# Softmax-free attention mixed with a state-space convolution: the denominators of the last stage in a PSUM bank, with copies in SBUF

## The chip, the cores and the metric

The kernel runs on one core of a Trainium2 chip. The metric is the device time of one launch in microseconds (us). Before the change the median of three runs was 179.49 us (179.27 to 180.06).

The engines go by their short names in the profile: PE is TensorE (its weight loads are a row of their own, PEld), DVE is VectorE, ACT is ScalarE, POOL is GpSimd and SP is SyncE, which only issues DMAs here. A suffix q (ACTq, SPq) marks what the engine's sequencer does, such as issuing a DMA. Each engine works through its own list of instructions in order.

## The reference

The input x has 2048 rows of 448 numbers. Two branches are computed and mixed per row:

```
g   = sigmoid(x . gate_w)
q, k, v = split(x @ wqkv) into 16 heads of 28
phi(t)  = (t + 1 if t > 0 else exp(t)) + 1e-6
kv  = sum over rows of phi(k)^T v          # 28 x 28 per head
z   = sum over rows of phi(k)              # 28 per head
a   = (phi(q) @ kv) / (phi(q) . z + 1e-6) @ wo
b   = long convolution of x along the rows (S4D kernel) + x * D_skip
out = g * a + (1 - g) * b
```

The denominators of this case are the 16 numbers `phi(q) . z + 1e-6` of every row, one per head.

## The kernel before, in words

The rows are cut into 16 blocks of 128 (`NC = 16`); a block lies with its rows on the 128 partitions. All instructions are written out in the order in which each engine is to do them (`manual_schedule`), so the order of the Python lines that name one engine is that engine's order. Tile pools decide only the buffers: a tile with the tag of an earlier one waits until the last reader of that one is done.

The first part (to line 507) takes block after block: project k, make phi(k), accumulate the products `g` of phi(k) with x in four PSUM banks, project q, make phi(q) (`pq`), and the convolution branch `y`. While the last block passes, z is summed over the partitions by a matmul and copied to `zb` (L629).

Then comes a bridge (L630 to L741). ACT copies the four banks `g` to SBUF (`gs`, L646). PE multiplies them with the weights of v (L691, in two parts `k` and `tr`; each part goes through the four copies in turn for one block of heads, then through them again for the next), DVE masks the result (`kv`), ACT and DVE split it into a high and a low half, and PE multiplies with wo (L671, tiles m0 to m3). ACT takes the high half of each m (`m_high`, L675, into `wk` or `shl`), DVE the low half (L679). Four small DMAs move rows of `shl` into `wk` (L725, L726); one of them is issued from ACT's list.

The last stage is a loop over the 16 blocks (L766 to L789). For block c:
- `norm_a` (L517): POOL multiplies `pq` with `zb` into `prod`, two buffers.
- `norm_b` (L522): DVE sums `prod` over the 28 columns of each head, into `den`.
- `norm_d` (L527, L529): DVE adds 1e-6, multiplies with `e1` (from the gate) and takes the reciprocal, in the loop for two blocks at once, in every second pass.
- `norm_c` (L540, L543, L546): `pn` is `pq` times the reciprocals; POOL does two pieces, DVE a small one of 48 columns.
- `turn_pe`, `turn_split` (L577, L584, L585): PE transposes `pn`, ACT takes the high half `th`, DVE the low half.
- `tail` (L588): ACT copies three gate rows of `rows` into the tile of `th`.
- `attend` (L602): PE multiplies the halves with `wk` and `rc`, 11 matmuls; the eighth takes `rc` and the rows that `tail` copied.
- `final_b`, `final_c` (L607, L609, L613): DVE adds `y`, SP sends the block out, ACT keeps a copy of the bank in `pq`.

`norm_bd(0)` to `norm_bd(3)` (reduce, then L527 and L529 for one block) and `norm_c(0)` to `norm_c(2)` stand in the bridge, between the pieces named above. The gates for the last stage are transposed by `gates_b` (L564) into a PSUM bank, copied by ACT (L567) and DVE (L568).

Of the kernel before, what the change touches and what calls it, by code (L numbers as in the profile page):

```python
# [7 lines left out]
F32 = mybir.dt.float32  # L8
# [3 lines left out]
ALU = mybir.AluOpType  # L12
AX = mybir.AxisListType
PSUM = bass.MemoryType.PSUM

P = 128
S = 2048
D = 448
H = 16
DH = 28  # L20
N = 256
NC = S // P
# [14 lines left out]
DS = 12  # L37
# [93 lines left out]
def gated_mix_kernel(ctx: ExitStack, tc: tile.TileContext, xin, wq_d, wv_d, wo_d, abc_d, ldt_d, dsk_d,  # L131
                     tri_d, ident_d, mask_d, gcat_d, sel_d, first_d, gin_d, lag_d, out):
    nc = tc.nc
    PE, ACT, DVE, POOL, SP = nc.tensor, nc.scalar, nc.vector, nc.gpsimd, nc.sync
# [39 lines left out]
    tp = work.enter_context(tc.tile_pool(name="tp", bufs=2))  # L174
    ps = work.enter_context(tc.tile_pool(name="ps", bufs=1, space=PSUM))
# [18 lines left out]
    o = 0  # L194
    for part in PARTS:
# [8 lines left out]
        o = e  # L204
# [305 lines left out]
    gs = [gs[i // 2][:, i % 2] for i in range(4)]  # L510
    mh, ml = wkh, wkl
    rc = []
    pn, th, tl, pd, dn = {}, {}, {}, {}, {}

    def norm_a(c):
        pd[c] = tp.tile([P, D], F32, name="prod", tag="pk")
        POOL.tensor_tensor(out=pd[c], in0=pq[:, c], in1=zb, op=ALU.mult)  # L517

    def norm_b(c):
        if c % 2 == 0:  # L520
            dn[c // 2] = tp.tile([P, 2, H], F32, name="den", tag="den", bufs=3)
        DVE.tensor_reduce(out=dn[c // 2][:, c % 2], in_=pd.pop(c).rearrange("p (h d) -> p h d", h=H), op=ALU.add,  # L522
                          axis=AX.X)

    def norm_d(c, n):
        r = dn[c // 2][:, c % 2:c % 2 + n]
        DVE.scalar_tensor_tensor(out=r, in0=r, scalar=1e-6, in1=e1[:, c:c + n, None].to_broadcast([P, n, H]),  # L527
                                 op0=ALU.add, op1=ALU.mult)
        DVE.reciprocal(out=r, in_=r)  # L529

    def norm_bd(c):
        norm_b(c)
        norm_d(c, 1)

    def norm_c(c):
        n = pn[c] = tp.tile([P, J, P], F32, name="pn", tag="pn")
        r = dn[c // 2][:, c % 2]
        a = pq[:, c, :3 * DJ].rearrange("p (j h d) -> p j h d", j=3, h=4)
        b = pq[:, c, 3 * DJ:].rearrange("p (h d) -> p h d", h=4)
        POOL.tensor_tensor(out=n[:, :3, :DJ].rearrange("p j (h d) -> p j h d", h=4), in0=a,  # L540
                           in1=r[:, :H - 4].rearrange("p (j h) -> p j h", j=3)[:, :, :, None].to_broadcast([P, 3, 4, DH]),
                           op=ALU.mult)
        DVE.tensor_tensor(out=n[:, :3, DJ:].rearrange("p j (h d) -> p h j d", h=4),  # L543
                          in0=b[:, :, :DS].rearrange("p h (j d) -> p h j d", j=3),
                          in1=r[:, H - 4:, None, None].to_broadcast([P, 4, 3, DS // 3]), op=ALU.mult)
        POOL.tensor_tensor(out=n[:, 3].rearrange("p (b h d) -> p b h d", b=2, h=4),  # L546
                          in0=b[:, None, :, DS:].to_broadcast([P, 2, 4, DH - DS]),
                          in1=r[:, None, H - 4:, None].to_broadcast([P, 2, 4, DH - DS]), op=ALU.mult)
# [11 lines left out]

    def gates_b(g, tag):
        n = g.shape[1]
        o = ps.tile([P, 512], F32, name="o2", tag="v1")
        PE.transpose(o[:n, :P], g, ident)  # L564
        w = tp.tile([P, D], F32R, name="phs", tag=tag)[:n, :3 * P].rearrange("p (i t) -> p i t", i=3)
        phs.append(w)
        ACT.copy(w[:, 0:2], o[:n, None, :P].to_broadcast([n, 2, P]))  # L567
        return lambda: DVE.tensor_tensor(out=w[:, 2], in0=o[:n, :P], in1=w[:, 0].bitcast(F32), op=ALU.subtract)  # L568
# [46 lines left out]
    c = NC - 2  # L615
# [18 lines left out]
    g2 = gates_a(1, NC - 1)  # L634
    POOL.memset(rows[DT:RX, :2 * D], 0.0)
    last = gates_b(g2, "pkl")
    DVE.tensor_copy(okn, zo[:1, D:D + 1])
    norm_bd(0)
    norm_c(0)
    last()  # L640
    norm_a(2)
    norm_bd(1)
    norm_c(1)
    for i in range(4):
        do_g(c + 1, (i,))
# [80 lines left out]
    SP.dma_start(out=mh[DT:, 3].bitcast(F32), in_=shl[:DT, 1].bitcast(F32))  # L726
    o0 = turn_pe(0)
    norm_c(2)
    norm_a(4)
    mrows(0, p3, "a")  # L730
# [11 lines left out]
    def late():  # L742
        c = NC - 1
        yield 5
        e = tp.tile([P, D], F32, name="e", tag="e")
        t = tp.tile([P, D], F32, name="t", tag="t")
        ACT.activation(e1[:, c:], qo[:, D:D + 1], AF.Exp, scale=-1.0)
        ACT.activation(e, qo[:, :D], AF.Exp)
        yield 6
        DVE.tensor_scalar(out=e1[:, c:], in0=e1[:, c:], scalar1=1.0, scalar2=None, op0=ALU.add)  # L750
        DVE.tensor_scalar(out=t, in0=e, scalar1=1.0, scalar2=1e-6, op0=ALU.min, op1=ALU.add)
        DVE.reciprocal(out=og[:, c:], in_=e1[:, c:])
        yield 7
        DVE.tensor_scalar(out=og[:, c:], in0=og[:, c:], scalar1=-1.0, scalar2=1.0, op0=ALU.mult, op1=ALU.add)
        DVE.scalar_tensor_tensor(out=pq[:, c], in0=qo[:, :D], scalar=C1, in1=t, op0=ALU.add, op1=ALU.max)
        yield 8
        g = gates_a(c, NC)
        yield 9
        last = gates_b(g, "e")
        yield 10  # L760
        last()
        phi(c)
# [3 lines left out]
    for c in range(NC):  # L766
        if c % 2 and c + 4 < NC:
            norm_d(c + 3, 2)
        if c:
            final_b(c - 1)  # L770
        if 0 < c < NC - 2:
            norm_c(c + 2)
        if c + 1 < NC:
            turn(c + 1)
        if c:
            final_c(c - 1)
        if c + 1 < NC:
            tail(c + 1)
        if c + 6 < NC:
            norm_a(c + 6)  # L780
        if c + 5 < NC - 1:
            phi(c + 5)
        attend(c, ((0, D // 2), (D // 2, D)) if c == NC - 1 else ((0, D),))
        if c == 0:
            norm_b(4)
        if c + 5 < NC:
            norm_b(c + 5)
        if c == due:
            due = next(later, None)  # L789
# [94 lines left out]
```

## Time and profile before

| | |
|---|---|
| median of three runs | 179.49 us (179.27 to 180.06) |
| the profiled execution | 179.93 us |
| its span | 178.1 us |
| PE busy | 172.5 us, 97% |
| DVE busy | 115.9 us, 65% |
| ACT busy | 94.7 us, 53% |
| POOL busy | 119.5 us, 67% |

The span runs from the first to the last recorded instruction; 1.83 us of the profiled execution lie outside it. Rows of the timeline read: start in us, busy time in us, engine, line, operation, output tile, input tiles, count, and in brackets the idle time of that engine just before and what ended it. Buffer numbers are left out of the names. The chain of work that ended last is PE for 91% of the span.

### The profile page before, as it was taken

How to read it: one execution, taken by the hardware profiler on the slowest of the kernel's cores; microseconds unless marked ns; L12 is line 12 of the kernel's file. 1: busy time of each engine (PE TensorE's matmuls, PEld its weight loads, DVE VectorE, ACT ScalarE, POOL GpSimd, SP SyncE). 2: the span in 40 equal slices, each digit the busy share in tenths (PEclk: the TensorE clock that was granted, in tenths of full speed). 3: DMA queues.
4: the chain of work that ended last, by engine and by line, in shares of the span. 5: the costliest groups of instructions: out<-in, count | busy, mean ns of one | idle time of the engine just before them, and what ended most of it. 6: DMA issues, size and time to landing. Idle time of an engine off the chain costs nothing.

```text
span 178.1 us, 2750 instructions
## 1 busy us (share of the span) xinstructions
PE 172.5 (97%) x879; PEld 152.0 (85%) x879; DVE 115.9 (65%) x238; ACT 94.7 (53%) x212; POOL 119.5 (67%) x124
## 2 busy tenths in 40 slices
PE   6999999999999999999999999999999999999991
PEld 2598999999999999999989999877879999899990
DVE  1747647688857173562824519389799999998551
ACT  3779388884537244372536653444565455564441
POOL 3167577879259969687598999059289998773100
PEclk9999999999999999999999999999999999999999
DMA  5999974198003303033033000000031221131222
GB/s 166 416 291 271 249 203 153 10 375 239 4 1 118 118 0 120 5 118 101 18 118 122 0 0 0 0 4 5 6 60 68 88 98 62 67 119 73 109 76 82
DMA packets 7784, 18.40 MB, mean 103 GB/s; under 512 B 1755, under 2 KB 4520, under 8 KB 7768
## 3 DMA queue, kind: packets, MB, share of 16 engines
q1 hardware_dynamic: 7720, 18.16, 32.2%
q8 instruction: 7, 0.11, 0.3%
q10 hardware_dynamic: 48, 0.06, 0.2%
q14 instruction: 9, 0.07, 0.1%
HBM read 14.20 MB, written 3.67 MB: 100 GB/s over the span
## 4 chain that ended last, share of the span: by engine, by line
PE 91%; DVE 5%; issue 1%; ACT 1%; ACTq 0%
PE g L388 20%; PE q L319 19%; PE a L602 16%; PE k L319 15%; PE v L319 6%; PE tr L577 3%; PE q L246 3%; PE v L396 2%; PE v L395 2%; PE m L671 1%; DVE th L585 1%; DVE ot L607 1%; DVE den L527 1%; DVE den L522 1%; PE tr L691 1%
## 5 line engine op out<-in xcount | busy, mean ns | idle before, releaser
L602 PE MATMUL a<-wk,th 128*128 128x448 f32 (+1 forms) x170 | 39.5, 364 | 0.0
L388 PE MATMUL g<-pkh,xn 128*128 128x448 f32 x112 | 36.1, 370 | 0.0
L602 PEld LDWEIGHTS a<-wk,th 128*128 128x128 f32 x170 | 29.6, 189 | 2.6 <-DMA wk<-shl 0.3
L319 PE MATMUL k<-wk,xt 128*128 128x448 f32 x132 | 30.4, 376 | 0.0
L347 DVE SCALAR_TENSOR_TENSOR k<-k,e 128x448 f32<-128x448 f32 x12 | 7.6, 632 | 33.9 <-ACT e L346 33.9
L319 PE MATMUL q<-wqh,xt 128*128 128x450 f32 x120 | 27.7, 368 | 0.0
L319 PEld LDWEIGHTS k<-wk,xt 128*128 128x128 f32 x132 | 25.1, 190 | 2.9 <-ACT wk L416 0.8
L407 POOL TENSOR_TENSOR y<-y,t 128x448 f32<-128x448 f32 x16 | 18.6, 1163 | 13.4 <-DVE t L400 13.1
L224 POOL TENSOR_TENSOR xn<-xr,xn 128x448 fp32r<-128x448 f32 x16 | 19.2, 1200 | 8.7 <-ACT xn L234 8.4
L319 PEld LDWEIGHTS q<-wqh,xt 128*128 128x128 f32 x120 | 22.7, 189 | 2.7 <-issue 0.7
L517 POOL TENSOR_TENSOR prod<-pq,zb 128x448 f32<-128x448 f32 x16 | 18.6, 1162 | 8.3 <-ACT zb L629 6.0
L388 PE MATMUL g<-pkl,xn 128*128 128x448 f32 x64 | 23.5, 367 | 0.0
L388 PEld LDWEIGHTS g<-pkh,xn 128*128 128x128 f32 x112 | 21.1, 188 | 2.8 <-issue 0.2
L345 ACT ACTIVATE e<-k 128x448 f32<-128x448 f32 x12 | 6.5, 545 | 30.2 <-PE k L319 30.2
L240 POOL TENSOR_TENSOR y<-xr,rows 128x448 f32<-128x448 f32 x16 | 18.7, 1168 | 0.0
L224 POOL TENSOR_TENSOR xt<-xr,xt 128x512 fp32r<-128x512 f32 x14 | 18.3, 1306 | 0.2 <-ACT xt L228 0.2
L540 POOL TENSOR_TENSOR pn<-pq,den 128x336 f32<-128x336 f32 x16 | 12.1, 754 | 7.7 <-DVE den L529 5.6
L584 ACT CAST th<-tr 128x512 fp32r<-128x512 f32 x16 | 9.4, 589 | 9.2 <-PE tr L577 9.0
L607 DVE SCALAR_TENSOR_TENSOR ot<-y,og,a 128x448 f32<-128x448 f32 (+1 forms) x17 | 10.4, 615 | 4.6 <-PE a L602 4.6
L613 ACT COPY pq<-a 128x448 f32<-128x448 f32 (+1 forms) x17 | 8.8, 517 | 6.5 <-DVE ot L607 5.7
L388 PEld LDWEIGHTS g<-pkl,xn 128*128 128x128 f32 x64 | 11.2, 175 | 1.2 <-issue 0.2
L319 PE MATMUL q<-wql,xt 128*128 128x450 f32 x45 | 11.7, 364 | 0.0
(135 smaller groups left out, 305.0 us busy)
## 6 DMA issues: line engine op xcount, KB each, us to landing
xr<-in SPq DMA_DIRECT2D x15, 512.0 KB, 3.5
out<-ot SPq DMA_DIRECT2D x15, 224.0 KB, 1.9
pq<-in SPq DMA_DIRECT2D x4, 448.0 KB, 13.3
y<-in SPq DMA_DIRECT2D x2, 480.0 KB
y<-in SPq DMA_DIRECT2D x2, 450.0 KB, 7.4
wv<-in SPq DMA_DIRECT2D x1, 896.0 KB, 5.5
wo<-in SPq DMA_DIRECT2D x1, 784.0 KB
y<-in SPq DMA_DIRECT2D x1, 448.0 KB
```

What stands on the lines that cost most here:

```text
L224: eng.tensor_tensor(out=o, in0=r, in1=h.bitcast(F32), op=ALU.subtract)
L240: POOL.tensor_tensor(out=y[:, c], in0=plain[c][:, :D], in1=dsk, op=ALU.mult)
L319: PE.matmul(o[:, :n], lhsT=a, rhs=b, start=run.n == 1, stop=not seq)
L347: DVE.scalar_tensor_tensor(out=pks[c], in0=pks[c], scalar=1.0, in1=e, op0=ALU.add, op1=ALU.max)
L388: PE.matmul(g[i][:a.shape[1], :D], lhsT=a, rhs=b, start=c == 0 and n == 0, stop=c == NC - 1 and n == len(seq) - 1)
L407: POOL.tensor_tensor(out=y[:, c], in0=y[:, c], in1=t, op=ALU.add)
L517: POOL.tensor_tensor(out=pd[c], in0=pq[:, c], in1=zb, op=ALU.mult)
L540: POOL.tensor_tensor(out=n[:, :3, :DJ].rearrange("p j (h d) -> p j h d", h=4), in0=a, in1=r[:, :H - 4].rearrange("p (j h) -> p j h", j=3)[ ...
L584: ACT.copy(h, ov)
L602: PE.matmul(a[:, lo:hi], lhsT=u_, rhs=w_[:, lo:hi], start=n == 0, stop=n == 10)
L607: DVE.scalar_tensor_tensor(out=ot[:, lo:hi], in0=y[:, c, lo:hi], scalar=og[:, c:c + 1], in1=a[:, lo:hi], op0=ALU.mult, op1=ALU.add)
L613: ACT.copy(pq[:, c, lo:hi], a[:, lo:hi])
```

## The change

The change has three parts. The sums of all 16 blocks go into one PSUM tile `dp`, in the bank with tag v1, where they stay: the sum, the 1e-6, the gate factor and the reciprocal are computed there. After each reciprocal ACT copies the result into the old SBUF tile `den`, since POOL reads `den` in `norm_c` from SBUF. DVE's small piece of `norm_c` reads `dp`. The transposed gates of `gates_b` move from the bank v1 to the bank q.

```
     def norm_b(c):
-        if c % 2 == 0:
-            dn[c // 2] = tp.tile([P, 2, H], F32, name="den", tag="den", bufs=3)
-        DVE.tensor_reduce(out=dn[c // 2][:, c % 2], in_=pd.pop(c).rearrange("p (h d) -> p h d", h=H), op=ALU.add,
-                          axis=AX.X)
+        if not dp:
+            dp.append(ps.tile([P, 512], F32, name="den", tag="v1")[:, :NC * H].rearrange("p (c h) -> p c h", c=NC))
+        DVE.tensor_reduce(out=dp[0][:, c], in_=pd.pop(c).rearrange("p (h d) -> p h d", h=H), op=ALU.add, axis=AX.X)
 
     def norm_d(c, n):
-        r = dn[c // 2][:, c % 2:c % 2 + n]
+        r = dp[0][:, c:c + n]
         DVE.scalar_tensor_tensor(out=r, in0=r, scalar=1e-6, in1=e1[:, c:c + n, None].to_broadcast([P, n, H]),
                                  op0=ALU.add, op1=ALU.mult)
         DVE.reciprocal(out=r, in_=r)
+        if c % 2 == 0:
+            dn[c // 2] = tp.tile([P, 2, H], F32, name="den", tag="den", bufs=3)
+        ACT.copy(dn[c // 2][:, c % 2:c % 2 + n], r)
...
         DVE.tensor_tensor(out=n[:, :3, DJ:].rearrange("p j (h d) -> p h j d", h=4),
                           in0=b[:, :, :DS].rearrange("p h (j d) -> p h j d", j=3),
-                          in1=r[:, H - 4:, None, None].to_broadcast([P, 4, 3, DS // 3]), op=ALU.mult)
+                          in1=dp[0][:, c, H - 4:, None, None].to_broadcast([P, 4, 3, DS // 3]), op=ALU.mult)
...
-        o = ps.tile([P, 512], F32, name="o2", tag="v1")
+        o = ps.tile([P, 512], F32, name="o2", tag="q")
```

Lines behind the new ones are two higher in the changed kernel (L646 becomes L648, L675 becomes L677, L588 becomes L590). The order of PE, DVE, POOL and SP is the same; ACT has ten copies more (L531).

ACT's list at the start of the bridge, before: the copy of the gates, then the four copies of `g`, then `zs` for another matmul.

```order
L567 CAST phs<-o_1254 14x256 [waits PE_49]
L646 COPY gs_1182<-g_142 128x448 [waits PE_49,Pool_49]
L646 COPY gs_1182<-g_143 128x448 [waits PE_49]
L646 COPY gs_1183<-g_144 128x448 [waits PE_49,Pool_49]
L646 COPY gs_1183<-g_145 128x448 [waits PE_49]
```

The same place after:

```order
L569 CAST phs<-o_1254 14x256 [waits PE_49]
L531 COPY den<-den 128x16 [waits DVE_49] x2
L648 COPY gs_1182<-g_142 128x448 [waits PE_49,Pool_49]
L648 COPY gs_1182<-g_143 128x448 [waits PE_49]
L648 COPY gs_1183<-g_144 128x448 [waits PE_49,Pool_49]
L648 COPY gs_1183<-g_145 128x448 [waits PE_49]
```

The copies of the reciprocals of blocks 0 and 1 stand ahead of the four copies of `g`, and each waits for DVE.

ACT's list later in the bridge, before, from the high half of m3 (`shl`) to the transposed block 1:

```order
L675 CAST shl<-m_1339 112x448 [waits PE_49]
L675 CAST wk_69<-m_1349 112x448 [waits PE_49]
L725 DMA wk_69<-shl 16x2x448 [waits DVE_49]
L675 CAST wk_69<-m_1370 112x448 [waits PE_49]
L675 CAST wk_69<-m_1376 112x448 [waits PE_49]
L584 CAST th<-tr 128x512
L735 CAST wk_69<-shl 64x448
L736 CAST rc<-shl 64x448
L588 CAST th<-rows 48x128 [waits DVE_49,Pool_49]
L584 CAST th<-tr 128x512 [waits PE_49]
```

The same place after:

```order
L677 CAST shl<-m_1342 112x448 [waits PE_49]
L531 COPY den<-den 128x16 [waits DVE_49]
L677 CAST wk_69<-m_1353 112x448 [waits PE_49]
L727 DMA wk_69<-shl 16x2x448 [waits DMAHW6_49,Activation_49]
L677 CAST wk_69<-m_1374 112x448 [waits PE_49]
L677 CAST wk_69<-m_1380 112x448 [waits PE_49]
L586 CAST th<-tr 128x512
L737 CAST wk_69<-shl 64x448
L738 CAST rc<-shl 64x448
L531 COPY den<-den 128x16 [waits DVE_49]
L590 CAST th<-rows 48x128 [waits Pool_49]
L586 CAST th<-tr 128x512 [waits PE_49]
```

The copy for block 2 stands ahead of the high half of m2, of ACT's DMA and of all that follows; the copy for block 3 stands ahead of the rows of block 0 (L590).

DVE's list in the loop for the second pass (c = 1), after; in the program before, the row of `pn` there has no wait:

```order
L526 SCALAR_TENSOR_TENSOR den<-den,e_60 128x32 [waits DVE_49]
L528 RECIPROCAL den<-den 128x32 [waits DVE_49]
L609 SCALAR_TENSOR_TENSOR ot<-y,og,a 128x448 [waits PE_49]
L545 TENSOR_TENSOR pn<-pq,den 128x4x3x4 [waits Activation_49]
L587 TENSOR_TENSOR th<-tr,th 128x512 [waits Activation_49]
```

DVE's piece of `pn` now waits for ACT's copy out of the same bank, which in turn waits for the reciprocal.

More of the change, by code (lines that the diff above doesn't have):

```diff
@@ L512, in gated_mix_kernel @@
     rc = []
-    pn, th, tl, pd, dn = {}, {}, {}, {}, {}
+    pn, th, tl, pd, dn, dp = {}, {}, {}, {}, {}, []
     def norm_a(c):
```

## The prediction

> **What bounds the kernel now.** I read the summary first, then the stretches of the last stage, then the chain of work that ended last.
>
> ```profile
> PE 172.5 (97%) x879; PEld 152.0 (85%) x879; DVE 115.9 (65%) x238; ACT 94.7 (53%) x212; POOL 119.5 (67%) x124
> ...
> 145.00:150.00 5.00, 5.00 (x30) 4.56 (x29) 5.00 (x12) 3.09 (x8) 4.60 (x7) 1.00 0.26 96
> 150.00:155.00 5.00, 4.77 (x27) 4.13 (x26) 4.96 (x13) 2.13 (x5) 3.50 (x5) 1.00 0.12 46
> ...
> 151.93 0.56 DVE pn L543
> 152.49 0.14 issue
> 152.62 0.63 PE tr L577 x4
> ```
>
> PE is busy 97% of the span, so whatever holds PE is paid in full, and whatever only frees another engine is paid back only where PE stands idle. In the last stage DVE is full as well (5.00 of 5.00 us from 145 to 150). Only once does it show: from 150 to 155 PE is busy 4.77 of 5.00 us, and the chain names the place, the transposes of block 9, which start at 152.62 because DVE's piece of `pn` ended late. That stall is 0.23 us.
>
> **What the change removes.** DVE's small operations on `den` have long and short instances.
>
> ```profile
> L527 DVE SCALAR_TENSOR_TENSOR den<-den,e x10: 170/358/1073, 119.5 to 160.9; 128x32 f32<-128x32 f32 x6, 128x16 f32<-128x16 f32 x4
> L543 DVE TENSOR_TENSOR pn<-pq,den x16: 194/534/1165, 120.3 to 167.0; 128x48 f32<-128x48 f32 x16
> ```
>
> The same 48 columns take 194 ns or 1165 ns; 16 or 32 columns take 170 to 1073 ns. The longest L527 stands beside a product of POOL:
>
> ```profile
> 149.78 1.30 POOL L517 TENSOR_TENSOR prod<-pq,zb 128x448 f32<-128x448 f32 x1 [0.20 <-DVE e L750]
> ...
> 150.06 1.07 DVE L527 SCALAR_TENSOR_TENSOR den<-den,e 128x32 f32<-128x32 f32 x1
> ```
>
> It ends at 151.13, when the product has just ended (151.08). So I read the long ones as held by POOL's instructions on two SBUF operands; with `dp` in PSUM they have one SBUF input left. DVE operations that read one PSUM and one SBUF operand show no such spread in this stage (L607, L585: 0.58 to 0.69 us each), so I take the short times for all: 10 x (358 - 170) + 16 x (534 - 194), by medians, is some 7 us of DVE time. Of this PE can get back the 0.23 us at 152.62 and hardly more; DVE's freed time beyond it is time in which DVE waits for PE. The gain is bounded by zero and the idle time of PE and its weight loads in this stage, 0.8 us (this stall, and 0.25 and 0.34 us at 130.8 to 131.4, shown below, which the profile puts down to a copy and a DMA). I take 0.23.
>
> **What the change adds: a first hold on ACT.** Ten copies alone are small. Their nearest rows are these, a PSUM source with one column and an SBUF source with 128:
>
> ```profile
> L365 ACT ACTIVATE e<-q x14: 162/171/177, 20.7 to 115.4; 128x1 f32<-128x1 f32 x14
> L588 ACT CAST th<-rows x16: 294/295/297, 130.7 to 171.0; 48x128 fp32r<-48x128 f32 x16
> ```
>
> A copy of 16 or 32 columns lies between 0.17 and 0.295 us; I take 0.20, near the row from PSUM. But each waits for a reciprocal, ACT works in order, and the first two stand ahead of the four copies of `g` that PE needs.
>
> ```profile
> 119.44 2.19 ACT L646 COPY gs<-g 128x448 f32<-128x448 f32 x4 [0.29 <-PE g L388]
> 119.53 0.45 DVE L527 SCALAR_TENSOR_TENSOR den<-den,e 128x16 f32<-128x16 f32 x1
> 120.01 0.25 DVE L529 RECIPROCAL den<-den 128x16 f32<-128x16 f32 x1
> 120.30 0.21 DVE L543 TENSOR_TENSOR pn<-pq,den 128x48 f32<-128x48 f32 x1
> 120.42 0.27 DVE L568 TENSOR_TENSOR phs<-o,phs 14x128 fp32r<-14x128 f32 x1
> 120.62 0.60 DVE L522 TENSOR_REDUCE den<-prod 128x16 f32<-128x448 f32 x1
> 121.25 0.45 DVE L527 SCALAR_TENSOR_TENSOR den<-den,e 128x16 f32<-128x16 f32 x1
> 121.74 0.25 DVE L529 RECIPROCAL den<-den 128x16 f32<-128x16 f32 x1
> 122.14 1.73 PE L691 MATMUL k<-gs,wv 128*112 128x112 f32 x16
> 123.70 1.74 PE L691 MATMUL tr<-gs,wv 128*112 128x112 f32 x16
> 124.23 0.20 DVE L704 TENSOR_TENSOR kv<-k,mask 112x48 f32<-112x48 f32 x1
> ```
>
> Before, ACT starts `gs` at 119.44 and is done at 121.63, just ahead of PE's use at 122.14. After, block 0: 119.53 + 0.17, reciprocal 0.25, the gaps of 0.03 to 0.05 us between dependent rows, and the copy 0.20 end at 120.2; DVE's `pn`, which now waits for that copy, starts no later than its old 120.30, so the reduce of block 1 stays at 120.62 (its `prod` is there only at 119.94 anyway). Block 1: 121.25 + 0.17 and 0.25 give 121.70, the copy ends at 121.95. The saving of 0.28 us on DVE is in this. Then `gs`: 121.95 + 2.19 = 124.14 instead of 121.63, 2.5 us late. PE takes 16 passes in (123.70 - 122.14) = 1.56 us, 0.098 us each, two for a product; the fourth copy is first needed by passes 7 and 8, so ten passes lie behind it: 124.19 + 0.98 = 125.17 for the start of `tr`, against 123.70. **PE is 1.47 us late**, and the DVE and ACT work on kv behind it with it, since it starts when PE ends.
>
> [...]
>
> **A second hold.** Block 2's copy stands ahead of the high half of m2.
>
> ```profile
> 126.74 0.54 ACT L675 CAST wk<-m 112x448 fp32r<-112x448 f32 x1
> ...
> 127.53 0.71 ACTq L725 DMA_DIRECT2D wk<-shl  x1
> ...
> 128.27 0.25 DVE L529 RECIPROCAL den<-den 128x16 f32<-128x16 f32 x1
> 128.28 0.97 ACT L675 CAST wk<-m 112x448 fp32r<-112x448 f32 x2 [1.00 <-DVE den L527]
> ...
> 129.13 0.60 ACT L584 CAST th<-tr 128x512 fp32r<-128x512 f32 x1
> ...
> 129.96 0.68 DVE L585 TENSOR_TENSOR th<-tr,th 128x512 fp32r<-128x512 f32 x1
> ...
> 130.56 0.61 DVE L679 TENSOR_TENSOR wk<-m,wk 112x448 fp32r<-112x448 f32 x1
> 130.73 0.29 ACT L588 CAST th<-rows 48x128 fp32r<-48x128 f32 x1
> 130.80 0.30 PEld L602 LDWEIGHTS a<-wk,th 128*128 128x128 f32 x2 [0.25 <-ACT rc L736]
> ...
> 131.09 0.60 DVE L522 TENSOR_REDUCE den<-prod 128x16 f32<-128x448 f32 x1
> 131.44 0.91 PEld L602 LDWEIGHTS a<-wk,th 128*128 128x128 f32 x5 [0.34 <-DMA wk<-shl]
> 131.77 1.16 POOL L517 TENSOR_TENSOR prod<-pq,zb 128x448 f32<-128x448 f32 x1 [0.86 <-DVE den L522]
> 131.94 0.25 DVE L529 RECIPROCAL den<-den 128x16 f32<-128x16 f32 x1
> ...
> 132.37 0.19 PEld L602 LDWEIGHTS a<-rc,th 112*128 112x128 f32 x1
> ```
>
> The reciprocal of block 2 ended at 128.52; 1.47 later is 129.99. Copy 0.25 with its wait: the high half of m2 starts at 130.24, not 126.74 + 1.47 = 128.21, and ends at 130.78. Then comes ACT's DMA, whose issue holds ACT for 0.71 us, and the next high half starts at 131.53 instead of 128.28: ACT is 3.25 late, DVE's `th` of block 0 starts at 133.01 instead of 129.96 (3.05), the low half and the reduce behind it likewise, and the reciprocal of block 3 ends at 132.19 + 3.05 = 135.24. Its copy ends at 135.49, and only then may ACT copy the rows for block 0: 135.5 + 0.29 = 135.8 (130.73 before). PE's eighth matmul of block 0 needs them: weight load at 135.9 instead of 132.37. **PE is 3.5 us late**, 1.47 of it from the first hold, 2.0 from the second. The DMA alone (issue at 130.8, 3.27 us late against 127.53) would hold PE's second matmul, near 131.0 before, to 134.3, which is covered.
>
> POOL adds a little. It waits for the reduce of block 3 (0.86 us at 131.77) and then for that of block 4, behind the `th` of block 1; its `pn` of block 3, just in time for PE before (135.87 for 135.91), comes some 3.7 late. I add 0.2.
>
> **The rest.** In the loop the copies stand ahead of `th` in every second pass, behind a reciprocal; DVE has L607 (0.58) to do until its `pn` needs the copy (0.25), so this costs PE nothing as long as DVE keeps the ease that the first part gives. The gates in the bank q are read off at 120.69, and the q matmuls behind them start at 121.83: 1.1 us of cover. The bank v1 is free when DVE's reduce first writes it. After 136 the order is as before and PE is full, so nothing gives the delay back except the 0.23 us.
>
> **Sum:** 1.47 + 2.0 + 0.2 - 0.23 = 3.5 us (rounded). On the profiled execution, 179.93, this is 183.4; it lies 0.44 above the median of the runs, so on the median 179.49 + 3.5 = **183.0 us**. Copies of 0.17 to 0.295 us (three on the path), the gap to POOL and the DMA move this to 182.4 to 183.9.
>
> **Rivals.**
> - Only the first hold reaches the end: `wk` and the rows have more room than I see, and PE's q matmuls (2 us from 128.3) hide the second. For it: before, ACT waited 1.00 us for nothing but its own DMA there. Against it: PE already waited for DMA and `rc` at 130.8 and 131.4. 179.49 + 1.47 - 0.23 = 180.7. Chance 0.14.
> - The other side, not slower: DVE's freed 7 us starts work earlier than PE's stalls show, and the bridge's stalls of 0.25 and 0.34 us go too. It decides if block 1's reciprocal were ready by 119.44, when ACT starts `gs`; against it, `prod` of block 1 ends at 119.94. 179.49 - 0.8 = 178.7, and a little lower if PE has idle time that the rows hide. Chance 0.05; without any hold and with the 0.23 alone, 179.3, chance 0.04.
> - A third hold in the loop: DVE's `pn` waits for ACT's copy out of the same bank. [...] If the copy falls behind `th` (0.59 us) or `pq`, six passes lose some 0.2 us each: 184.2. It decides where DVE's work of two passes, some 4.9 us, passes PE's two blocks of 2.69 us (5.38). Chance 0.12.
> - The change doesn't do what it says: the long instances stay long with a PSUM operand. Then block 1's copy is 0.28 later, the 0.23 stays, and a full DVE adds to it: 184 us. Chance 0.07.
>
> **Chances and range.** My forecast has 0.58, the rivals 0.42. Faster by over 0.5% (0.9 us, about what a measurement of this kernel can tell from no change) has 0.03, the lower part of the second rival; within it 0.06, the rest of that rival and the 179.3; slower 0.91. The range reaches to the first rival below and the third above: 180.7 to 184.3.
>
> **What would show it.** In the profile after: `gs` starting near 122.0 behind two copies L531; the first product of `tr` near 125.2; the high half of m2 near 130.2; the weight load of `rc` near 135.9 with ACT's row copy ahead of it; the transposes of block 9 without a wait for DVE; L526 and L545 all near 0.2 us. I am wrong if ACT reaches `gs` before 121, if PE has idle time after 140 that I don't name, or if the end moves by less than the bridge does.

## The result and the profile after

The changed kernel takes 182.59 us, the median of four runs (182.25 to 183.19); the kernel before took 179.63 (179.27 to 180.06) beside it. The ratio is 1.0175 [1.0157, 1.0193], with the 95% interval in brackets: slower by 2.8 to 3.5 us.

The summary of the changed kernel, and the three stretches of its last stage that answer to the ones shown of before (columns: stretch, its length, busy time of PE, PEld, DVE, ACT and POOL with instruction counts, granted clock, DMA share, GB/s):

```profile
PE 173.1 (96%) x879; PEld 151.9 (84%) x879; DVE 110.3 (61%) x238; ACT 95.5 (53%) x222; POOL 119.4 (66%) x124
```

```profile
130.00:135.00 5.00, 3.56 (x18) 2.55 (x17) 3.33 (x8) 3.30 (x8) 3.04 (x5) 1.00 0.22 49
145.00:150.00 5.00, 5.00 (x30) 4.58 (x29) 4.14 (x9) 3.04 (x10) 5.00 (x8) 1.00 0.25 92
150.00:155.00 5.00, 5.00 (x29) 4.56 (x28) 4.53 (x15) 2.73 (x7) 4.32 (x7) 1.00 0.27 95
```

The reader sees both halves of the change here. DVE is relieved: 110.3 us busy against 115.9, no longer full from 145 to 150, and PE has no gap from 150 to 155, where it had one. The price is paid from 130 to 135, at the end of the bridge, where PE is busy 3.56 of 5.00 us.

DVE's small operations of the changed kernel, each line with its shortest, median and longest instance, and ACT's ten copies:

```profile
L526 DVE SCALAR_TENSOR_TENSOR den<-den,e x10: 176/183/200, 119.0 to 162.8; 128x32 f32<-128x32 f32 x6, 128x16 f32<-128x16 f32 x4
L545 DVE TENSOR_TENSOR pn<-pq,den x16: 191/196/205, 119.7 to 169.1; 128x48 f32<-128x48 f32 x16
L531 ACT COPY den<-den x10: 172/185/187, 119.5 to 163.4; 128x32 f32<-128x32 f32 x6, 128x16 f32<-128x16 f32 x4
```

The long instances are gone: L526 reaches 200 ns where L527 reached 1073, L545 reaches 205 where L543 reached 1165.

The chain of work that ended last, in the changed kernel, begins in the bridge (start, us, what):

```profile
129.73 0.50 issue
130.23 0.97 ACT wk L677 x2
131.20 0.49 ACT th L586
...
131.75 0.57 issue
132.32 0.61 DVE wk L681
132.94 0.55 DVE den L522
...
134.22 0.29 ACT th L590
...
137.75 0.52 DVE ot L609
138.26 0.12 DVE pn L545
138.38 0.14 issue
138.52 0.63 PE tr L579 x4
```

Before, the chain could be followed back through the whole program, and PE was 91% of the span. Now it can be followed back to 129.73 only; ACT and DVE carry it by turns from there to 138.5, and PE takes over at the transposes of block 3. That is the stretch in which the time is lost.

**A common zero.** In the profiled run of the changed kernel all of the bridge starts 0.53 us earlier than before, as ACT's copy of `zb` shows (first row before, second row after):

```profile
117.07 0.53 ACT L629 COPY zb<-zo 128x448 f32<-128x448 f32 x1 [1.07 <-PE zo L627]
```

```profile
116.54 0.53 ACT L631 COPY zb<-zo 128x448 f32<-128x448 f32 x1 [1.07 <-PE zo L629]
```

That copy starts between 116.42 and 117.24 in the fourteen profiles of this study, though only one edit touches the code ahead of it; it is the scatter of the first part. So I subtract its start from every time. This table has, from that zero, the weight load of `rc` for block 0 (PE's eighth matmul), the transposes of block 3, the pitch from the transposes of block 8 to those of block 9, the start of ACT's last copy out of the banks, and then the time from there to the end of the span. The names are those of the experiments below.

| kernel | `rc` load | block 3 | pitch 8 to 9 | last copy | to the end |
|---|---|---|---|---|---|
| before | 15.30 | 19.01 | 3.07 | 57.72 | 3.31 |
| after | 18.02 | 21.98 | 2.69 | 60.28 | 3.88 |
| loop_only | 15.46 | 19.18 | 2.70 | 57.47 | 3.31 |
| hold01 | 16.48 | 20.19 | 2.69 | 58.47 | 3.89 |
| hold2 | 15.61 | 19.87 | 2.69 | 58.22 | 3.33 |
| hold3 | 15.80 | 19.75 | 2.69 | 58.07 | 3.33 |
| copies_sbuf | 18.32 | 22.63 | 3.45 | 61.76 | 3.34 |
| sum_psum | 15.46 | 19.17 | 2.69 | 57.46 | 3.36 |

### The profile page after: what moved, and what is told of

Read it like the earlier page. It is cut to its first block, busy times and chain, and to the rows that moved or that the text cites. A ratio compares the mean times of both kernels' runs of the same rounds, so it can differ in the third digit from the quotient of the medians.

```text
span 180.7 us, 2775 instructions
## 1 busy us (share of the span) xinstructions
PE 173.1 (96%) x879; PEld 151.9 (84%) x879; DVE 110.3 (61%) x238; ACT 95.5 (53%) x222; POOL 119.4 (66%) x124
## 5 line engine op out<-in xcount | busy, mean ns | idle before, releaser
L319 PE MATMUL k<-wk,xt 128*128 128x448 f32 x132 | 29.7, 369 | 0.0
L407 POOL TENSOR_TENSOR y<-y,t 128x448 f32<-128x448 f32 x16 | 18.6, 1165 | 13.4 <-DVE t L400 13.1
L319 PEld LDWEIGHTS k<-wk,xt 128*128 128x128 f32 x132 | 24.6, 188 | 3.2 <-ACT wk L416 0.5
L587 DVE TENSOR_TENSOR th<-tr,th 128x512 fp32r<-128x512 f32 x16 | 11.1, 691 | 4.5 <-ACT th L586 4.1
```

Of the source, the lines that this page charges most:

```text
L319: PE.matmul(o[:, :n], lhsT=a, rhs=b, start=run.n == 1, stop=not seq)
L407: POOL.tensor_tensor(out=y[:, c], in0=y[:, c], in1=t, op=ALU.add)
L587: DVE.tensor_tensor(out=l, in0=ov, in1=h.bitcast(F32), op=ALU.subtract)
```

## The experiments

My theory: the whole loss is the place of the four bridge copies on ACT's list, and the whole gain is DVE's short operations, which is worth one stall of PE. The rivals: ACT's copies in the loop cost too; the PSUM operands or the shared bank cost by themselves; only the first hold reaches the end.

**loop_only** leaves the denominators of blocks 0 to 3 in SBUF, with no ACT copy, and does the rest as changed.

```
+    OLD = (0, 1, 2, 3)
...
-        ACT.copy(dn[c // 2][:, c % 2:c % 2 + n], r)
+        if c not in OLD:
+            ACT.copy(den(c)[:, c % 2:c % 2 + n], r)
```

> Blocks 0 to 3, whose denominators are made in the bridge, as in the kernel before (SBUF, no copy by ACT); blocks 4 to 15 as in the change. If the loss is the copies that hold ACT in the bridge, nothing is lost and the stall before block 9 is gone: 0.2 to 0.4 us under the kernel before, 179.1 to 179.4. If the PSUM operands or the copies in the loop cost as well, 180 or more.

Measured: 179.09 us, ratio to before 0.998 [0.9966, 0.9994]. The loss is gone, and a gain of about 0.35 us is left. PE's transposes of blocks 8 to 10 in this kernel:

```profile
149.06 0.60 PE L589 MATMUL tr<-ident,pn 128*128 128x128 f32 x4
151.76 0.60 PE L589 MATMUL tr<-ident,pn 128*128 128x128 f32 x4
154.45 0.60 PE L589 MATMUL tr<-ident,pn 128*128 128x128 f32 x4
```

The steps are 2.70 and 2.69 us: the stall at block 9 is gone. Six ACT copies in the loop, each behind a reciprocal and out of the bank that DVE reads next, cost nothing that shows.

**copies_later** keeps all of the change, and moves only the four bridge copies down ACT's list: behind the copies of `g`, behind `rc`, and behind the `th` of block 1. `norm_c(0)` to `norm_c(2)`, which need the copies, move down with theirs; the cut shows the first two.

```
-    norm_c(0)
...
-    norm_c(1)
...
+    for i in range(2):
+        norm_e(i, 1)
+        norm_c(i)
```

> All of the change, but the four copies of the bridge stand behind what they held: those of blocks 0 and 1 behind the four copies of g, that of block 2 behind the copy of rc, that of block 3 behind the high half of block 1. If only the place on ACT's list costs, 179.1 to 179.5. If the copies or the wait of DVE's pn for them cost wherever they stand, 180.5 or more.

Measured: 179.16 us, 0.9982 [0.997, 0.9993], the same as loop_only. With ten ACT copies and every denominator in PSUM, nothing is lost. So the place on the list was the cost.

**twice** is loop_only with DVE writing the reciprocal a second time, to SBUF, in place of ACT's copy.

```
-            ACT.copy(den(c)[:, c % 2:c % 2 + n], r)
+            DVE.reciprocal(out=den(c)[:, c % 2:c % 2 + n], in_=r)
```

> As loop_only, and DVE itself writes the reciprocal a second time, to SBUF, in place of ACT's copy. DVE has room for 0.37 us more in two passes (5.4 us), so 179.1 to 179.5, like loop_only. If DVE is still the bound in the loop, 180 or more.

Measured: 179.16 us, 0.998 [0.9969, 0.999]. With and without ACT's copies in the loop the time is the same, so the rival of a third hold falls.

**gates_q** is the kernel before with only the gates moved to the bank q.

```
-        o = ps.tile([P, 512], F32, name="o2", tag="v1")
+        o = ps.tile([P, 512], F32, name="o2", tag="q")
```

> The kernel before, with nothing but the transposed gates in the bank of q. The gates are read 1.1 us before PE writes that bank again, so no difference: 179.4 to 179.8. If that bank costs a wait, PE's first q matmul of the bridge comes late and the time grows by as much.

Measured: 179.56 us, 1.0009 [0.9998, 1.0021]: no effect, as the prediction had it.

**copies_sbuf** is the kernel before with ACT's ten copies at the change's places, from SBUF to SBUF; nothing goes to PSUM.

```
+        ACT.copy(dc[c // 2][:, c % 2:c % 2 + n], r)
...
-        r = dn[c // 2][:, c % 2]
+        r = dc[c // 2][:, c % 2]
```

> The kernel before (denominators in SBUF), with ACT copying each reciprocal to a second SBUF tile that POOL reads, at the same places as in the change. If the places on ACT's list are the cost, it loses as much as the change or more, since DVE's long instances stay and make the reciprocal of block 1 later: 182.5 to 184. If PSUM as such is the cost, 179.5 to 180.

Measured: 183.66 us, 1.022 [1.0199, 1.024]. The holds come without any PSUM, as ACT's list in this kernel shows:

```profile
120.22 0.20 ACT L532 COPY denc<-den 128x16 f32<-128x16 f32 x1 [1.15 <-DVE den L529]
121.95 0.21 ACT L532 COPY denc<-den 128x16 f32<-128x16 f32 x1 [1.53 <-DVE den L529]
122.07 1.83 ACT L649 COPY gs<-g 128x448 f32<-128x448 f32 x4
```

And the long instances remain (up to 1068 and 1161 ns), on a DVE that now runs late. Its waits (engine, line, what it waited for: us in total, times, longest) have a row that grew from 0.2 us:

```profile
PE tr L580 <- DVE pn L546: 1.1, 2, 0.6
```

Its last copy comes 61.76 - 60.28 = 1.5 us later than in the changed kernel; by the ratios of the whole times it is 0.8 us, since the changed kernel loses some 0.5 us again behind that copy. So beside the holds the PSUM bank is worth 1.5 us up to the last copy, and without them only some 0.3.

**hold01, hold2 and hold3** are loop_only with blocks 0 and 1, block 2, or block 3 done as in the change.

```
-    OLD = (0, 1, 2, 3)
+    OLD = (2, 3)
```

> As loop_only, but blocks 0 and 1 as in the change, so the first hold alone. The profile of the change has PE 1.1 us late at the products of tr, so about 1.1 over loop_only: 180.1 to 180.5. If the first hold is hidden by a later wait of the bridge, 179.2.

> As loop_only, but block 2 as in the change. The reciprocal of block 2 is ready at 128.5, so the high half of m2 comes 2.0 us late, the next ones 1.5, and PE's first matmuls of block 0 wait for th and for ACT's DMA: 0.5 to 0.9 us over loop_only, 179.7 to 180.1. If q matmuls hide it, 179.2.

> As loop_only, but block 3 as in the change. Its reciprocal ends at 132.2, the rows of block 0 then at 132.8 against PE's need at 132.4: 0.4 to 0.8 us over loop_only, 179.6 to 180.0. If the hold only costs behind the two others, 179.2.

Measured: hold01 180.89 us, 1.0069 [1.0044, 1.0093]; hold2 180.22 us, 1.0037 [1.0023, 1.0052]; hold3 179.85 us, 1.0011 [0.9997, 1.0026]. Over loop_only, by the ratios, these are 1.6, 1.0 and 0.6 us. hold3 is where it was expected; hold2 came out just above its range (179.7 to 180.1), and hold01 0.4 us above (180.1 to 180.5). In the table, hold01's last copy is 58.47 - 57.47 = 1.0 us late, as expected, and the other 0.58 us lie behind that copy, which no theory had foreseen. hold2 and hold3 cost 0.75 and 0.60 at the last copy. The weight loads show how they do it. In hold2 the load of `rc` (first row) did not wait, and the transposes of block 3 (second row) did:

```profile
132.36 0.19 PEld L614 LDWEIGHTS a<-rc,th 112*128 112x128 f32 x1
...
136.61 0.50 PEld L589 LDWEIGHTS tr<-ident,pn 128*128 128x128 f32 x4 [0.76 <-POOL pn L552]
```

In hold3 both waited:

```profile
132.60 0.19 PEld L614 LDWEIGHTS a<-rc,th 112*128 112x128 f32 x1 [0.35 <-ACT th L600]
...
136.52 0.42 PEld L589 LDWEIGHTS tr<-ident,pn 128*128 128x128 f32 x4 [0.52 <-POOL pn L552]
```

So the rows for block 0 can be late for their own reason (hold3), but most of the delay of block 2's copy reaches PE by another way when it is alone, and not by the first matmuls of block 0, as I had expected: ACT's halves are late, so DVE's reduce is, so POOL's `prod` and `pn` of block 3 are. The three add up to 3.2 of the 3.5 us by which the whole change is behind loop_only; the intervals reach some 0.25 to 0.45 us to each side, so the rest is not separable.

**sum_psum** has sums and the gate factor of all blocks in PSUM, and DVE writes the reciprocal straight to SBUF: no copy, and `pn` reads SBUF.

```
-        DVE.reciprocal(out=r, in_=r)
...
-        ACT.copy(dn[c // 2][:, c % 2:c % 2 + n], r)
+        DVE.reciprocal(out=dn[c // 2][:, c % 2:c % 2 + n], in_=r)
```

> All blocks: sum and L526 in the PSUM bank, the reciprocal written by DVE straight to SBUF, where POOL and DVE's pn read it; no copy by ACT, no wait for one. L526 is short, pn keeps its long instances. Before block 9 the longest L527 (1.07 us) goes, which is more than the stall of 0.23: 179.1 to 179.4, as good as loop_only. If the long pn make the stall, 179.5.

Measured: 179.15 us, 0.997 [0.9956, 0.9984]. Its two small DVE lines:

```profile
L528 DVE SCALAR_TENSOR_TENSOR den<-den,e x10: 173/183/200, 119.5 to 160.5; 128x32 f32<-128x32 f32 x6, 128x16 f32<-128x16 f32 x4
L546 DVE TENSOR_TENSOR pn<-pq,den x16: 199/348/1006, 120.1 to 166.8; 128x48 f32<-128x48 f32 x16
```

`pn` is as uneven as before, and yet the pitch at block 9 is 2.69 us. So a short gate factor alone ends the stall. It also moves the `pn` of block 9, though: here that one takes 0.20 us (at 151.12, in the last 0.03 us of POOL's product), where it took 0.55 before.

**pn_psum** is the other half: sums in SBUF, the reciprocal written twice, `pn` reads PSUM.

```
+        DVE.reciprocal(out=dp[0][:, c:c + n], in_=r)
...
-                          in1=r[:, H - 4:, None, None].to_broadcast([P, 4, 3, DS // 3]), op=ALU.mult)
+                          in1=dp[0][:, c, H - 4:, None, None].to_broadcast([P, 4, 3, DS // 3]), op=ALU.mult)
```

> All blocks: sum and L527 in SBUF as before, with their long instances; DVE writes the reciprocal twice, to PSUM for its own pn and in place for POOL. pn is short. Before block 9 pn gives back 0.36 us, enough for the stall of 0.23, but the second reciprocal takes as much: 179.3 to 179.7, no change. If pn alone makes the stall, 179.1.

Measured: 179.7 us, 1.0006 [0.9994, 1.0019]: no change.

```profile
L531 DVE SCALAR_TENSOR_TENSOR den<-den,e x10: 170/381/1076, 118.9 to 160.6; 128x32 f32<-128x32 f32 x6, 128x16 f32<-128x16 f32 x4
L548 DVE TENSOR_TENSOR pn<-pq,den x16: 145/197/198, 119.9 to 166.8; 128x48 f32<-128x48 f32 x16
```

Here the short line is `pn` and the long one is the gate factor. From the zero, the transposes of blocks 8 and 9 start at 33.11 and 35.91, a pitch of 2.80: most of the stall goes this way too. But those of block 3 start at 19.62, 0.45 later than in sum_psum, and the last copy at 58.06. DVE has the long gate factor and a reciprocal more, and what the stall gives is spent at block 3. The time came out as expected; the place where the gain is lost, block 3 and not block 9, did not.

**all_twice** is the whole change with DVE's second reciprocal in place of all ten ACT copies.

```
-        ACT.copy(dn[c // 2][:, c % 2:c % 2 + n], r)
...
+        DVE.reciprocal(out=dn[c // 2][:, c % 2:c % 2 + n], in_=r)
         DVE.reciprocal(out=r, in_=r)
```

> All blocks: sum and L526 in PSUM, DVE writes the reciprocal twice, to SBUF for POOL and in place for its own pn; both kinds of long instances are gone, ACT has no copy. PE is the bound of the bridge and the loop, so no better than loop_only: 179.0 to 179.3. If DVE's stretched operations of the bridge cost PE something, below 178.9.

Measured: 179.37 us, 0.9983 [0.9968, 0.9997]. That is just above the expected 179.3, but beside its own runs of before (179.69) it is the gain of loop_only again. Of the five faster kernels (loop_only, copies_later, twice, sum_psum, all_twice) sum_psum, with the fewest operations, has the lowest ratio, though their intervals overlap.

**more_code** is the whole change with five small DVE operations and four small ACT copies on an unused tile at the start of the program. It asks whether the 0.57 us at the end hang on where the code of DVE and ACT lies.

```
+    spare = const.tile([P, 4], F32, name="spare")
+    DVE.memset(spare, 0.0)
+    for i in range(4):
+        DVE.tensor_scalar(out=spare[:, i:i + 1], in0=spare[:, i:i + 1], scalar1=1.0, scalar2=None, op0=ALU.add)
+    for i in range(4):
+        ACT.copy(spare[:, i:i + 1], spare[:, i:i + 1])
```

> All of the change, and five small operations of DVE and four of ACT more at the very start, where both wait for the first DMA: they only move the code behind them. In the change and in hold01 the span ends 3.9 us after ACT's last copy starts, in all the others 3.3 us. If the place of the code does that, it is 3.3 here and the time 182.0; if it comes with the work or its late end, 3.9 and 182.6.

Measured: 181.8 us, 1.0116 [1.0093, 1.014]. Neither theory holds. The end is as long as in the changed kernel (3.82 us), and yet the time fell by 0.8 us by the medians. The profile shows 0.53 of it: the last copy starts 59.75 us from the zero against 60.28. 0.28 of that is there at the weight load of `rc` (17.74), and the rest comes from a pitch of 2.67 to 2.68 us a block instead of 2.69. I have no cause for either.

## Why the prediction was right, and which sizes were off

The side and the mechanism were right: 183.0 us was forecast, 182.59 measured, inside the range. The terms do not agree as well as the sum.

| step | predicted | measured |
|---|---|---|
| first hold, start of `tr` | 1.47 | 7.71 - 6.63 = 1.08 |
| second hold, load of `rc`, over the first | 2.0 | (18.02 - 15.30) - 1.08 = 1.64 |
| POOL, transposes of block 3 | 0.2 | (21.98 - 19.01) - 2.72 = 0.25 |
| the stall at block 9 | -0.23 | 2.69 - 3.07 = -0.38 |
| behind the last copy | none | 3.88 - 3.31 = 0.57 |
| sum | 3.5 | 3.16 |

The ratio gives 0.0175 x 179.63 = 3.14. Without the last term the forecast would have been 0.9 us too high; that it is 0.4 off is partly luck.

**First hold.** ACT's list in the changed kernel:

```profile
119.51 0.17 ACT L531 COPY den<-den 128x16 f32<-128x16 f32 x1 [0.84 <-DVE den L528]
121.20 0.17 ACT L531 COPY den<-den 128x16 f32<-128x16 f32 x1 [1.52 <-DVE den L528]
121.27 1.85 ACT L648 COPY gs<-g 128x448 f32<-128x448 f32 x4
...
129.13 0.17 ACT L531 COPY den<-den 128x16 f32<-128x16 f32 x1 [1.74 <-DVE den L528]
129.19 0.71 ACTq L727 DMA_DIRECT2D wk<-shl  x1
129.19 0.54 ACT L677 CAST wk<-m 112x448 fp32r<-112x448 f32 x1
130.23 0.97 ACT L677 CAST wk<-m 112x448 fp32r<-112x448 f32 x2 [0.50 <-issue]
...
134.02 0.17 ACT L531 COPY den<-den 128x16 f32<-128x16 f32 x1 [1.42 <-DVE den L528]
134.22 0.29 ACT L590 CAST th<-rows 48x128 fp32r<-48x128 f32 x1
```

The two copies stand where the step put them, and `gs` starts 4.73 us from the zero, 0.15 earlier than the forecast (121.95 - 117.07 = 4.88). But the four copies take 1.85 us, and I had carried over 2.19. The row of before was not a price of four copies: there ACT started `gs` while PE was still filling the banks, and copies_later, which starts them there again, shows 2.19 again. That the wait for PE makes the difference is my reading. These are 0.49 us; 0.10 go the other way, since `tr` starts 1.13 us after the end of the copies (124.25 against 121.27 + 1.85) where I had put 1.03. Together this is the 0.39 us that the first hold was too large.

**Second hold.** The next loads of PE in the changed kernel:

```profile
134.56 0.19 PEld L604 LDWEIGHTS a<-rc,th 112*128 112x128 f32 x1 [1.40 <-ACT th L590]
...
138.49 0.42 PEld L579 LDWEIGHTS tr<-ident,pn 128*128 128x128 f32 x4 [0.53 <-POOL pn L542]
```

The load of `rc` waits for the rows, as predicted, at 134.56 (from the zero 2.72 later than before, forecast 3.5). Of the 0.78 us between, 0.36 come with the smaller first hold (the reciprocal of block 2 ends 1.11 late, not 1.47). Two more were sized wrong. The copy and its wait were put at 0.25 us, and the half of m2 starts 0.06 us after the copy does. And "then comes ACT's DMA, whose issue holds ACT for 0.71 us" placed the issue behind that half; the rows have both at 129.19, so the next halves start 1.04 us after it and not 1.29.

**POOL.** The wait of 0.53 us for `pn` of block 3 is the one foreseen. The chain shown above names DVE's piece of `pn` as the last to arrive, at 138.38, so POOL and DVE are late together.

**The stall.** It went, as predicted, but the step back is 0.38 us, not the 0.23 of idle time that the row of before named. PE's rows ahead of the same transposes, those of block 9, in the changed kernel show why:

```profile
154.08 0.78 PE L604 MATMUL a<-wk,th 128*128 128x448 f32 x3
154.69 0.60 PE L579 MATMUL tr<-ident,pn 128*128 128x128 f32 x4
```

Without a wait the transposes start before the matmuls ahead of them have ended (154.69 against 154.08 + 0.78 = 154.86; the ends are the profile's). So the stall of before cost its idle time of 0.23 us and, by estimate from these rows, this overlap of 0.17 us too. The prediction took the two DVE lines together; either one shortened ends most of the stall, the gate factor (sum_psum) without a loss elsewhere. DVE's freed time was 5.6 us of busy time and not some 7, which no term of the sum used.

**The costs put at nothing.** ACT's copies in the loop (twice) and the move of the gates (gates_q) cost nothing. In the changed kernel DVE waits for ACT's copy in two places only:

```profile
ACT den L531 <- DVE den L528: 11.8, 10, 1.7
...
DVE pn L545 <- ACT den L531: 0.5, 2, 0.2
```

Both are in the bridge, ahead of `pn` of blocks 0 and 1. ACT's own 11.8 us of waiting cost PE something only where PE was behind it.

**PSUM operands and long instances.** The reciprocal rose from 253 to 266 ns for 16 columns, the shortest gate factor from 170 to 176, and `pn` has a median of 196 ns where the shortest from SBUF was 194. In these rows an operand in PSUM in place of SBUF costs 2 to 13 ns.

The long instances of before have one pattern. The longest `pn` shows it:

```profile
121.99 1.14 POOL L517 TENSOR_TENSOR prod<-pq,zb 128x448 f32<-128x448 f32 x1
122.03 1.17 DVE L543 TENSOR_TENSOR pn<-pq,den 128x48 f32<-128x48 f32 x1
```

POOL's product ends at 123.13, the `pn` at 123.20. Of the 26 gate factors (L527) and `pn` (L543) 18 took over 0.25 us, and all 18 end 0.03 to 0.07 us after the POOL instruction during which they started. Of the eight short ones five started while POOL ran nothing, one beside POOL's memset, and two in the last 0.13 us of a POOL instruction. DVE's lines with a single SBUF input show no such spread: in the kernel before the reduce (L522) took 597 to 621 ns, the one at 118.9 within POOL's products (117.68 to 119.94), and the reciprocal (L529) a mean of 253 ns for 16 columns and 354 for 32. In the two half kernels the line with an operand in PSUM is short and the other is not: at most 200 ns for the gate factor and up to 1006 for `pn` in sum_psum, at most 198 for `pn` and up to 1076 for the gate factor in pn_psum. That POOL holds an operation because both its inputs are in SBUF is the prediction's reading; these rows fit it, and none shows how it comes about.

**The rivals.** Only the first hold: hold01 stands at 180.89, the change at 182.59, so it falls. Not slower: block 1's reciprocal would have had to end by 119.44, and its copy started at 121.20; the gain without the holds is 0.35 us, not 0.8. The third hold falls by twice. That the long instances stay falls by L526 and L545.

**Still open** is the time behind the last copy. There the program has a branch and then a barrier of all engines. SP's drains in that barrier, before and after:

```profile
L880 SPq DRAIN  x3: 7/13/19, 177.3 to 177.9; - x3
```

```profile
L882 SPq DRAIN  x3: 7/13/114, 179.4 to 180.2; - x3
```

In the changed kernel SP stands still for 0.4 us between its first drain (179.40) and the second (179.79), and that one takes 114 ns; before, the two follow each other within 0.1 us. The profile puts the wait down to PE's sequencer, but PE's own drain stands at 176.4, long before. The same shows in hold01 and more_code, and in no other of the fourteen. Two explanations fall. One 8 KB packet more of q14, which the page lists as an instruction queue, lies inside the span in these three; but it starts at 180.43, after that drain, and in the other eleven it comes too, 0.3 to 0.6 us behind the end of the span. And the granted clock was 1.00 in hold01 and more_code until 0.5 us before the end, while loop_only, with the ordinary 3.31 us, had 0.50 for its last 1.5 us.

What the three have in common is in SP's own list: one event wait more at the DMA of the gate rows (the first row is before, the second after; x2 in the other ten, x3 in hold01 and more_code).

```profile
L554 SPq EVENT_SEMAPHORE  x2: 972/1244/1515, 119.8 to 159.5; - x2
```

```profile
L556 SPq EVENT_SEMAPHORE  x3: 17/28/1551, 120.1 to 161.4; - x3
```

more_code lengthened the lists of DVE and ACT and left SP's as it was, so it did not test this. That the longer list makes the gap is not shown: no run took the wait out. The three also share the two copies ahead of `gs` with the denominators in PSUM; copies_sbuf has such copies without PSUM, two event waits at that DMA, and ends after 3.34 us.

## What to carry to other kernels

A copy of 0.17 us cost what stood behind it on its engine's list: four such copies held back 3 us of work, and the same copies a few rows further down cost nothing (copies_later, 0.9982). Before moving a value to another engine, look up when its input is ready and what that engine has to do until then, or let the engine that made it write it where it is read. And the 5.6 us that were freed on DVE were worth only the stall of PE that they ended, 0.4 us.

## What the runs showed of the hardware

- A gate factor or `pn` of 16 to 48 columns on DVE took 170 to 1165 ns with two SBUF inputs (before). In that kernel each one over 0.25 us ended 0.03 to 0.07 us after the POOL instruction during which it started. With one of the inputs in PSUM they took at most 205 ns in the changed kernel, 200 in sum_psum and 198 in pn_psum, and the PSUM operand itself added 2 to 14 ns (`pn` 194 to 196, the gate factor 170 to 176, the reciprocal 253 to 266, the reduce into PSUM 604 to 618).
- In the changed kernel ACT started a copy before the one ahead of it had ended: at 121.27, beside a copy that ran from 121.20 to 121.37. It also issued a DMA (0.71 us, at 129.19) beside a copy that stood ahead of it on its list (0.54 us, at 129.19); the next copy started only after the issue, 0.04 us behind it before and 0.33 after the change.
- ACT's copies of 16 or 32 columns took 172 to 187 ns from PSUM (changed kernel) and 203 to 220 ns from SBUF (copies_sbuf).
- From ACT's last copy to the end of the span, branch and closing barrier included, it took 3.3 to 3.4 us in eleven of the kernels and 3.8 to 3.9 in the three whose SP list has one event wait more; the cause is not shown.
